# Engine orders rebuilt in a gated attention and feed-forward kernel, with order constraints of the scheduler removed

## The chip, the cores and the metric

The kernel runs on one core of a Trainium2 chip. The metric is the device time of one execution in microseconds (us); lower is better. All executions used here are fast, on a granted clock of 0.998 to 1.0; one execution of the kernel before, of 301.57 us at a clock of 0.853, is left out. A ratio is the mean time of one kernel's fast runs over the mean of the other's fast runs of the same rounds, so it is not quite the ratio of the medians quoted beside it. The *head* is the time before the first score fill, some 15 us. The *span* is what the profiler traces of an execution; the device time was 1.7 us longer in most executions.

## The reference, cut to what matters

```python
# x [1, 2048, 512] bf16, 32 heads of 16, 4 segments of 512 rows; feed-forward width 1792
g = sigmoid((x * gate_w).sum(-1))
for s in range(4):                       # attention with a running memory
    p     = softmax(q_s @ k_s.T * scale + causal_mask)
    a_dot = p @ v_s
    a_mem = (phi(q_s) @ M) / (phi(q_s) @ z + 1e-6)
    o_s   = sigmoid(beta) * a_mem + (1 - sigmoid(beta)) * a_dot
    M, z  = M + phi(k_s).T @ v_s, z + phi(k_s).sum()
a = concat(o_s) @ wo
b = (gelu(x @ w_gate) * (x @ w_up)) @ w_down
return g * a + (1 - g) * b
```

## The kernel before

The program is a set of named tasks. `qk2_1A0` fills the four score banks for one part of query tile 1 of segment 2 (a *fill*), `exp…` is its exponential on ScalarE, `pv` a P*V group, `mz` the memory group of a segment, `K Q V` projections, `G U D` pieces of the gate, up- and down-projection. A piece is two matmuls of 512 columns, 217 ns each from start to start. Pieces are matmuls of 128*128 by the trace's records (*full-array*); fills (32*128), P*V (128*17) and memory groups (128*32) consist of small matmuls (*tiled* work). The order of the tasks on each engine is a fixed list; a list scheduler in the source only plays it through, with its estimates of time, to choose PSUM banks. The semaphore waits are derived from what each task reads and writes.

```python
COLD = 5.8
BLOCK, BLOCK_ASK, BLOCK_END = 256, 165, 208
ORDER = {"pe": ("warm3 warm0 ... qk2_1B1 U2_4.0 U2_4.2 pv2_0_1 mz2 qk2_2A0 D1_3.10 ..."), ...}
HOP = {PE: 0.17, ...}
...
    # the scheduler, on TensorE: two instructions for each matmul
    n_ins = 2 * len(t.alts[PE])
    k = (done + n_ins - BLOCK_END) // BLOCK
    if done < BLOCK_END + BLOCK * k and k - 1 in fetched:
        t.finish = max(t.finish, fetched[k - 1] + ...)
    k = (done + n_ins - BLOCK_ASK) // BLOCK
    if done < BLOCK_ASK + BLOCK * k:
        fetched[k] = t.finish + max(0.8, min(dma_free - t.finish + 0.5, 4.0)) + 2.25
    done += n_ins
...
    for i in range(7):                                   # warm-up before the input has landed
        n = 512 if i < 6 else 384
        task(f"warm{i}", PE, [Instr(lambda e, gw=gw, n=n: e.matmul(
            gw.f32()[:, 0:n], ones[:, 0:128], ones[:, 0:n], start=True, stop=True), [], [gw.key], mm_t(n))], ...)
...
            for sm in sem_out + [sem_tail]:              # the last waits
                e.wait_ge(sm, 16)
```

The four lines around `BLOCK` matter later: the source holds an estimate of how TensorE's instructions arrive. Its figures are the source's own; what the runs show of them comes below.

The softmax here doesn't subtract the row's maximum and nothing guards it: scores larger than these inputs give would overflow.

## Time and profile before

| | before |
|---|---|
| time, median (lowest to highest) | 270.64 us (270.62 to 271.37, 3 runs); in the rounds beside the changed kernel 271.01 us (270.62 to 271.69, 6 runs) |
| span of the profiled run | 268.5 us |
| first score fill, last score fill | 14.79 us, 252.34 us |
| first score fill to end of the last matmul's issue | 250.72 us |
| stalls of TensorE in that stretch | 2.59 us, in 15 places of 0.07 to 0.41 us |
| work of TensorE after the last fill | 13.16 us |

A *stall* is a distance between two starts on TensorE above what the same step takes elsewhere: 217 ns for a matmul of 512 columns, 330 ns for a fill (345 for the low one), 664 ns for a P*V group, 640 ns for a memory group, 312 ns from a full-array matmul of 512 columns to the tiled work behind it, which is 95 ns above 217. The profile lines behind it are in the prediction.

### The profile page before, as it was taken

To read this page: it belongs to the slowest core of one execution; us is meant where nothing else is said; L and a number is where in the kernel's file an instruction comes from. 1 tells how busy PE (TensorE), PEld (TensorE's weight loads), DVE (VectorE), ACT (ScalarE), POOL (GpSimd) and SP (SyncE) were. 2 spreads that over 40 slices of the span, in tenths; PEclk is the share of its full clock that TensorE was granted. 3 is DMA by queue.
4 is the path that set the end of the run, shared out by engine and by line. 5 is a ranking of instruction groups with operands and counts; after the bars stand their busy time and mean duration, and the time that the engine had idled before them with its cause. 6 is when DMAs were issued, how large, how long until landed. Compare 5 with 4: busy or idle time off the path is not lost.

```text
span 268.5 us, 7148 instructions
## 1 busy us (share of the span) xinstructions
PE 263.2 (98%) x3017; PEld 118.9 (44%) x3017; DVE 199.4 (74%) x387; ACT 213.1 (79%) x188; POOL 106.4 (40%) x256
## 2 busy tenths in 40 slices
PE   8999999999999999999999999999999999999995
PEld 4634444344444435444444444443434443444453
DVE  1669888888897778878875987679787756667351
ACT  3899998989999697879968898778795886777702
POOL 8105876733000385253270342428470056344120
DMA  7954247334046135010000314210002023101002
GB/s 214 319 154 80 42 142 167 129 115 104 0 129 110 39 78 142 21 42 2 2 0 2 79 36 86 77 66 1 4 2 61 11 50 38 25 20 42 2 0 78
DMA packets 32815, 18.22 MB, mean 68 GB/s; under 512 B 20624, under 2 KB 32784, under 8 KB 32784
## 3 DMA queue, kind: packets, MB, share of 16 engines
q1 hardware_dynamic: 32208, 17.25, 25.4%
q8 instruction: 23, 0.38, 0.6%
q10 hardware_dynamic: 576, 0.52, 0.6%
q14 instruction: 8, 0.07, 0.1%
HBM read 9.84 MB, written 2.10 MB: 44 GB/s over the span
## 4 chain that ended last, share of the span: by engine, by line
PE 88%; ACT 9%; DMA 1%; issue 1%; POOL 0%; SPq 0%; ACTq 0%
PE psW L498 68%; PE psXALL L864 10%; ACT pt L871 7%; PE psW L914 5%; PE psXALL L498 3%; ACT ptl L871 1%; DMA wk<-in_A_wk_dram 1%; PE psW L922 1%; PE psW L830 1%; POOL ptl L875 0%; ACT ost L1050 0%; PE psXALL L596 0%; SPq L529 0%; ACTq L394 0%
## 5 line engine op out<-in xcount | busy, mean ns | idle before, releaser
L871 ACT ACTIVATE pt<-psXALL 128x2048 bf16<-128x2048 f32 x64 | 120.0, 1875 | 23.5 <-PE psXALL L864 21.4
L875 POOL TENSOR_SCALAR_AFFINE_SELECT pt<-pt 128x256 bf16<-128x256 bf16 x128 | 56.8, 454 | 67.2 <-ACT pt L871 62.4
L498 PE MATMUL psW<-xT,wu 128*128 128x512 bf16 x224 | 54.9, 380 | 0.0
L875 POOL TENSOR_SCALAR_AFFINE_SELECT ptl<-ptl 128x512 bf16<-128x512 bf16 x32 | 23.0, 719 | 77.3 <-ACT ptl L871 75.7
L498 PE MATMUL psW<-xT,wg 128*128 128x512 bf16 x224 | 53.6, 380 | 0.0
L498 PE MATMUL psW<-wd,hT 128*128 128x512 bf16 x210 | 52.5, 380 | 0.0
L1020 DVE TENSOR_TENSOR hT<-psW,hT 128x512 bf16<-128x512 f32 x56 | 36.9, 685 | 12.3 <-PE psW L498 12.1
L929 DVE STREAM_TRANSPOSE tb<-psW 128x512 f32<-128x512 f32 x32 | 21.9, 704 | 17.8 <-PE psW L922 17.5
L498 PEld LDWEIGHTS psW<-xT,wg 128*128 128x128 bf16 x224 | 20.4, 98 | 25.3 <-issue 2.3
L498 PEld LDWEIGHTS psW<-xT,wu 128*128 128x128 bf16 x224 | 20.2, 98 | 24.2 <-issue 2.3
L498 PEld LDWEIGHTS psW<-wd,hT 128*128 128x128 bf16 x210 | 18.6, 98 | 21.4 <-issue 3.0
L864 PE MATMUL psXALL<-qT,kpad 32*128 32x320 bf16 (+3 forms) x512 | 25.4, 273 | 1.4 <-ACT pt L871 0.8
L999 ACT ACTIVATE hT<-psW 128x512 bf16<-128x512 f32 x28 | 15.9, 601 | 7.5 <-PE psW L498 7.5
L871 ACT ACTIVATE ptl<-psXALL 128x2048 bf16<-128x2048 f32 x8 | 15.0, 1877 | 6.1 <-PE psXALL L864 6.0
L914 PE MATMUL psW<-pt,vaug 128*17 128x192 bf16 (+3 forms) x512 | 19.2, 273 | 0.0
L864 PEld LDWEIGHTS psXALL<-qT,kpad 32*128 32x128 bf16 x512 | 7.6, 92 | 24.3 <-ACT pt L871 17.2
L498 PE MATMUL psW<-wv,xT 128*128 128x512 bf16 x64 | 17.0, 380 | 0.0
L498 PE MATMUL psW<-xT,wk 128*128 128x512 bf16 (+1 forms) x80 | 16.7, 337 | 0.2 <-DMA wk<-in_A_wk_dram 0.2
L498 PE MATMUL psW<-wo,oT 128*128 128x512 bf16 x60 | 16.1, 380 | 0.0
L773 POOL COPY exsT<-exs 32x4 f32<-32x4 f32 x64 | 14.4, 225 | 3.7
L914 PEld LDWEIGHTS psW<-pt,vaug 128*17 128x17 bf16 x512 | 10.2, 90 | 12.5 <-issue 4.9
L515 DVE CAST hT<-psW 128x512 bf16<-128x512 f32 x17 | 11.4, 684 | 2.6 <-PE psW L498 2.6
(101 smaller groups left out, 312.7 us busy)
## 6 DMA issues: line engine op xcount, KB each, us to landing
out_dram<-ost SPq DMA_DIRECT2D x15, 128.0 KB, 1.9
wg<-in_B_w_gate_dram SPq DMA_DIRECT2D x2, 896.0 KB, 6.5
wu<-in_B_w_up_dram SPq DMA_DIRECT2D x2, 896.0 KB, 5.1
wd<-in_B_w_down_dram SPq DMA_DIRECT2D x2, 896.0 KB, 5.6
phkt<-in_A_x_dram SPq DMA_DIRECT2D x3, 512.0 KB, 3.6
vlow<-vaug SPq DMA_DIRECT2D x8, 136.0 KB, 2.7
wq<-in_A_wq_dram SPq DMA_DIRECT2D x2, 256.0 KB, 4.7
wv<-in_A_wv_dram SPq DMA_DIRECT2D x2, 256.0 KB, 5.3
```

Of the source, the lines that this page charges most:

```text
L498: return Instr(lambda e: e.matmul(view(), lhsT, rhs, start=first, stop=last), reads=reads, writes=[fkey if fkey is not None else g.key], e ...
L515: alts[DVE] = [Instr(lambda e: e.tensor_copy(dst(), src()), reads=reads, writes=writes, est=dve_t(n))]
L773: cross = task(f"exsT{s}", POOL, [Instr(lambda e, g=g, c=c: e.tensor_copy(exsT[sl][32 * g:32 * g + 32, c:16:4], exs[32 * c:32 * c + 32, s4 ...
L830: Instr(lambda e, t=t, kt=kt, c=c: e.matmul(gm.f32()[32 * c:32 * c + 32, 34 * t:34 * t + 34].rearrange("p (j e) -> p j e", e=17), phkt[:, ...
L864: instrs.append(Instr(lambda e, g=g, lhs=lhs, rhs=rhs, c0=c0, ncol=ncol: e.matmul(X[g][:, c0:c0 + ncol], lhs(32 * g), rhs(32 * g), start=T ...
L871: prev_exp[0] = exp_task(s, f"exp{s}_{t}{name}", [Instr(lambda e: e.activation(dst[:], XALL[:, :].rearrange("p (g c) -> p g c", g=4), ACTF ...
L875: task(f"msk{s}_{t}{name}", POOL, [Instr(lambda e, view=view, pat=pat, base=base: e.affine_select(out=view, in_=view, compare_op=ALU.is_ge ...
L914: instrs.append(Instr(lambda e, t=t, q=q, kb=kb, slot=slot, c0=c0: e.matmul(gp.f32()[32 * q:32 * q + 17, 128 * kb + 64:512], Vaug[sl][:, k ...
L922: instrs.append(Instr(lambda e, t=t, q=q, kb=kb, c0=c0: e.matmul(gp.f32()[32 * q:32 * q + 17, 128 * kb:128 * kb + 64], Vlow[j][:, kb, 4 * ...
L929: task(f"pvt{s}_{t}_{j}", DVE, [Instr(lambda e: e.transpose(Tb[:, j, :], gp.f32()[:, :]), [gp.key], [("Tb", j)], dve_t(512))], grp=gp)
L999: lambda e, g=g, ft=ft, s=s: e.activation(hT[s % 2][:, ft, :], g.f32()[:, :], ACTF.Gelu_apprx_tanh),
L1020: task(f"Um{s}_{ft}", DVE, [Instr(lambda e, g=g, ft=ft: e.tensor_tensor(hT[sl][:, ft, :], g.f32()[:, :], hT[sl][:, ft, :], ALU.mult), [g.k ...
```

## The change

The change frees the order of the tasks from constraints that the data do not ask for, gives new engine lists, corrects constants of the scheduler, and waits for the last 128-column piece of the output last.

```diff
-COLD = 5.8
+COLD = 4.9
 BLOCK, BLOCK_ASK, BLOCK_END = 256, 165, 208
 ORDER = {
-    ... qk2_1B1 U2_4.0 U2_4.2 pv2_0_1 mz2 qk2_2A0 D1_3.10 D1_3.12 D1_3.14 D1_1.0 D1_1.2 qk2_2B0 pv2_1_1 pv2_1_0 ...
+    ... K3_0.0 K3_0.2 qk2_2A0 U2_10.0 U2_10.2 pv2_1_1 mz2 pv2_1_0 qk2_2B0 D1_3.6 D1_3.8 V3_1.0 ...
     ... (the five lists, all rebuilt)
-HOP = {PE: 0.17, ...}
+HOP = {PE: 0.25, ...}
     ... (estimated sizes of ten input transfers)
-                    [("phkt", t), ("Vaug", sl, kt)], [gm.key], 0.009)
+                    [("phkt", t), ("Vaug", sl, kt)], [gm.key], 0.0115)
-                p = task(f"pv{s}_{t}_{j}", PE, instrs, grp=gp, after=joint)
+                p = task(f"pv{s}_{t}_{j}", PE, instrs, grp=gp)
-                mine[0].preds.add(lead)                 # gate groups of a segment, one after the other
-                                        kb == 3, 512) for kb in range(4)], 2, after=[gelu_of[s, ft]])
+                                        kb == 3, 512) for kb in range(4)], 2)
-            dep = hdep + (fins if last else [S._w[("oT", sl, tile, 3)]])
+            dep = fins if on_x else ()
-            for sm in sem_out + [sem_tail]:
+            for sm in sem_out[:-1] + [sem_tail, sem_out[-1]]:
                 e.wait_ge(sm, 16)
```

## The prediction

> **What bounds the kernel now.** I read the page first (engine shares, chain), then the waits, then the chain and the TensorE timeline where the chain leaves TensorE, and last the instruction records themselves, from which I took the start of every matmul and its distance to the next.

> ```profile
> span 268.5 us, 7148 instructions
> PE 263.2 (98%) x3017; PEld 118.9 (44%) x3017; DVE 199.4 (74%) x387; ACT 213.1 (79%) x188; POOL 106.4 (40%) x256
> ...
> PE 88%; ACT 9%; DMA 1%; issue 1%; POOL 0%; SPq 0%; ACTq 0%
> ```

> TensorE is busy 98% of the span and carries 88% of the chain; ScalarE carries 9%. Nothing else matters. The waits say what the 9% is: TensorE (its weight loads) waits for the exponentials that empty the four score banks, and ScalarE waits for the scores that fill them.

> ```profile
> ACT pt L871 <- PE psXALL L864: 21.4, 42, 0.8
> PEld psXALL L864 <- ACT pt L871: 18.0, 42, 0.8
> ```

> A weight load runs ahead of its matmul, so these 18.0 us are mostly hidden. Where they are not, the chain passes through the exponential (last segment):

> ```profile
> 221.83 0.44 PE psXALL L864 x8
> ...
> 222.35 1.89 ACT pt L871
> 224.24 0.05 issue
> 224.28 0.50 PE psXALL L864 x8
> ...
> 224.87 1.89 ACT pt L871
> 226.76 0.05 issue
> 226.80 0.51 PE psXALL L864 x8
> ...
> 227.39 1.89 ACT pt L871
> ```

> Score fills follow each other here at 224.28 and 226.80: 2.52 us, which is the shortest period the single set of score banks allows (exponential 1.89, hop 0.05, fill and hop 0.5 to 0.6). TensorE had less than that to do in between:

> ```profile
> 224.28 0.40 PE L864 MATMUL psXALL<-qT,kpad 32*128 32x320 bf16 x8 [0.17 <-ACT pt L871]
> 224.61 1.04 PE L498 MATMUL psW<-xT,wu 128*128 128x512 bf16 x4
> 225.49 0.59 PE L498 MATMUL psW<-wd,hT 128*128 128x512 bf16 x2
> 226.01 0.61 PE L914 MATMUL psW<-pt,vaug 128*17 128x448 bf16 x16
> 226.45 0.29 PE L922 MATMUL psW<-ptl,vlow 128*17 128x64 bf16 x16
> 226.80 0.40 PE L864 MATMUL psXALL<-qT,kpad 32*128 32x448 bf16 x8
> ```

> Six full-array matmuls and one P*V group end at 226.67 or so; the fill waits for the exponential that ends at 226.75.

> **What TensorE's time consists of.** From the records I took start-to-start distances: 217 ns on average after a 512-column matmul (713 pairs), 60 ns after one of 136 columns, one fill of the four score banks 330 ns (345 for the low fill), one P*V group 664 ns, two in a row 1217 ns for both (so 553 for the first), a memory group 640 ns, and 107 ns lost each time a full-array matmul is followed by a fill or a group. Counting the program's order with these: 1033 full-array matmuls 205.6 us; 77 entries into tiled work 8.2; 72 fills 23.9; P*V groups 22 x 664 + 10 x 553 = 20.1; 3 memory groups 1.9; sum 259.7 us. Measured from the first matmul (0.84) to the end of the last one's issue (265.50) are 264.7 us. The difference of 5.0 us has two parts. The head: warm-up matmuls 427 ns apart instead of 216, then waits for the first rows of wk, 2.4 us. Stalls later: 1.7 us in the steps from full-array work to a fill above the 107 ns, 0.6 us in steps from P*V to a fill that took up to 797 ns instead of 664, 0.15 us at 196.8 us, and 0.2 us in memory groups beside a P*V group (up to 751 ns); about 2.5 us in all. After the last matmul come 0.6 us of eviction, the output transfer (issued 266.39, landed 268.00) and the final waits: 2.9 us.

> So everything that an order of instructions can still win is 2.5 us of stalls, some tenths in the head, and a part of the 259.7. That is at most 1.2% of the time.

> [...] a 512-column matmul counts 380 ns, yet the next starts after 217, so 98% busy hides the stalls above and I used starts. [...] The kernel gives four to the scores and four to everything else; this limits how early an up-projection may start, as it holds its bank until its gelu is there.

> **The change part by part.** *Order constraints removed.* They are arguments of the scheduler only; the orders are fixed lists, and semaphore waits are derived from the data, so no instruction and no necessary wait disappears. They matter by what they allow: an up-projection before its gelu, a down-projection that starts with the hidden tiles that are ready, P*V groups two in a row. *Engine orders.* The same 625 TensorE tasks. The number of entries into tiled work is 77 again; P*V groups that directly precede another group rise from 10 to 13, so 3 x 111 ns = 0.33 us go: 259.4 us. *Spacing of the fills.* With the costs above I summed the TensorE work between each fill and the next. A fill period under 2.52 us (2.46 if full-array work precedes the fill, since 217.23 to 219.69 is such a pair) leaves TensorE waiting. Before there are 13 such intervals, 8 of them in the last segment, from 2.16 to 2.49 us; their deficits sum to 1.6 us of the 2.5 us measured. After there are three: 2.37 us (fill 1_1B1 to 1_2A0), 2.18 (3_2L to 3_2A1), 2.40 (3_3A1 to 3_3B1), deficits 0.09 + 0.28 + 0.06 = 0.43 us. The work that fills them is taken from the end: after the last fill 11.7 us of TensorE work remain instead of 13.1. So 1.6 - 0.43 = 1.2 us go. *The other 0.9 us of stalls* come from an exponential that starts late: at 188.31 one started 0.87 us after its fill instead of 0.59, and in the first segment copies sit between exponentials (57 to 63 us). The new lists move copies into longer intervals (3.58 us where three copies follow one exponential), so I let a third of it go, 0.3 us. *Head.* A seventh K-projection matmul hides part of a wait for the second half of the input (landed at 5.59 and 5.79): 0.1 us. All four first evictions are now on VectorE, 0.4 us each, in time for their readers by my count. *Tail.* One of the four last evictions goes to VectorE; the last piece's eviction did not wait in the trace (0.12 us after its matmul), so nothing is won. *Final waits.* The profile has them in pairs, the 384-column piece's last but one; waiting for the 128-column piece last may let one more already satisfied wait (0.06 us each in the trace) come after the landing: +0.06 us. *Model constants* (cold start, hop, transfer sizes) reach no instruction except through the choice of banks.
> Sum: 0.33 + 1.2 + 0.3 + 0.1 - 0.06 = 1.9 us. 270.64 - 1.9 = 268.8 us, 0.7% less.

> **Rivals.** *A: bank waits take the place.* Gates and up-projections are now opened earlier and hold banks longer: before the fourth fill (around 22 us) I count four open groups, one waiting for VectorE until about 22.7 us, just when the next group wants a bank. For: VectorE is 74% busy, and the slack there is about zero by my count. Against: in the trace of before, which has equally dense stretches, just one bank-like stall (0.14 us at 196.8) shows. It would cost 0.5 to 1.5 us and leave 269.3 to 270.3. *B: the fill period is ScalarE's, not TensorE's.* If the evictions moved between exponentials (two or three of 0.59 us) make ScalarE the bound in the first segment, stalls of 0.1 to 0.4 us appear at each; intervals of 2.60 us with a 1.05 us exponential task of the feature map in between need 2.85 us, but each is followed by one of 2.95 or more. Result 269 to 269.5. *C: all stalls vanish* and the head gains: 267.7 at the least. *D: transfers.* The memory group of the first segment moves from 38.6 to about 33 us; its transposes landed at 33.65. VectorE finishes their source some 3 us earlier by the new list, so they should land near 30.5; if not, TensorE stalls up to 1 us there.

> **Range and chances.** From C at 267.7 to A and D together at 270.3; the runs of before spread by 0.3% at most. I take 267.8 to 270.1. A change of 2% (5.4 us) is twice all that is idle, so faster than that has 1%; slower by 2% would need a blocked order, 1%.

> **What would show it right or wrong.** Right: steps from full-array work to a fill of 107 ns nearly throughout, the last fill some 1.5 us earlier relative to the end, the period of score fills in the last segment 2.6 us with ScalarE's wait for scores up and TensorE's for the exponential down; chain share of the exponentials from 7% to some 3%. Wrong: TensorE waiting for evictions (VectorE or ScalarE tiles) at 20 to 25 or 65 to 75 us, a wait for the transposed features near 33 us, or a fresh stall at the start of the down-projections.

0.33 + 1.2 + 0.3 + 0.1 - 0.06 us come to 1.87, its 1.9 us, and 270.64 less that is its 268.8 us. How far a weight load runs ahead of its matmul can be read in the trace of the kernel before: it starts 214 ns earlier in the median of the full-array matmuls and 27 ns in that of the tiled ones, at most 217 ns. What the rivals would cost are estimates.

## The result

The changed kernel took 269.83 us (median of 6; 268.92 to 270.22), the kernel before 271.01 us in the same rounds. The ratio is 0.9951, with a 95% interval of 0.993 to 0.9973: within 2%, and inside the predicted range. The predicted 268.8 us was 1.0 us too low.

These are the engine and chain shares of the changed kernel's page:

```profile
span 268.1 us, 7137 instructions
...
PE 262.9 (98%) x3017; PEld 118.9 (44%) x3017; DVE 200.7 (75%) x390; ACT 208.8 (78%) x184; POOL 105.9 (39%) x256
...
PE 96%; ACT 2%; issue 1%; DVE 0%; ACTq 0%
```

TensorE now carries 96% of the chain (the work that ended last, followed back) instead of 88%, and ScalarE 2% instead of 9%. The view of the waits, for the same two pairs as before and one further row (engine, line, tile, what was waited for: us in all, times, longest):

```profile
ACT pt L871 <- PE psXALL L864: 24.8, 41, 2.4
...
PEld psXALL L864 <- ACT pt L871: 17.4, 41, 0.6
...
PEld psXALL L864 <- issue: 3.8, 7, 1.3
```

ScalarE waits 3.4 us more for scores and TensorE's weight loads 0.6 us less for exponentials, which is the intended exchange. The last row is not intended. In the kernel before it is 3.0 us, 7 times, at most 0.4; now one score fill has a weight load that waited 1.3 us for "issue", that is for nothing the profile shows. The chain in the last segment, where the kernel before went through an exponential every 2.52 us (start, us, engine, tile and line, instructions):

```profile
217.41 0.33 PE psXALL L864 x8
217.74 2.27 PE psW L498 x10
220.00 0.33 PE psXALL L864 x8
220.33 2.26 PE psW L498 x10
222.60 0.33 PE psXALL L864 x8
```

Fills come every 2.60 us with ten full-array matmuls between them, and here the chain no longer leaves TensorE. Between the first fill and the last matmul it passes through an exponential only three times, at 105.5, 238.6 and 251.4 us, which are the three short intervals that the prediction had counted. The shortest, before fill 3_2A1:

```profile
238.11 0.48 PE psXALL L864 x32
238.59 0.02 issue
238.61 1.89 ACT ptl L871
240.50 0.05 issue
240.54 0.40 PE psXALL L864 x8
```

The stalls of the changed kernel in the stretch from first fill to last matmul are 0.14 us at 107.4, 0.06 at 152.0, 1.33 at 174.8, 0.19 at 197.7, 0.06 at 230.3, 0.32 at 240.5 and 0.13 at 253.3; in all 2.24 us. Without the third they are 0.91 us. That third one is here, in TensorE's timeline of the changed kernel (start, us, engine, line, operation, tiles, shape, count, in brackets the idle time before it and its releaser):

```profile
172.13 0.81 PE L830 MATMUL psW<-vaug,phkt 128*32 128x34 bf16 x64
172.77 0.63 PE L914 MATMUL psW<-pt,vaug 128*17 128x448 bf16 x16
173.21 0.30 PE L922 MATMUL psW<-ptl,vlow 128*17 128x64 bf16 x16
173.44 0.31 PE L864 MATMUL psXALL<-qT,kpad 32*128 32x320 bf16 x3
174.79 0.37 PE L864 MATMUL psXALL<-qT,kpad 32*128 32x320 bf16 x5 [1.04 <-issue]
```

Three of eight matmuls of one fill, then nothing for a microsecond, then the other five. The profile names no releaser, and in the program that the source builds only the first matmul of this fill carries a semaphore wait, so data and banks do not explain it. In front of it stand P*V, memory group, P*V and fill in one row, with no full-array matmul between: 272 instructions of TensorE, weight loads included, in about 2 us. The queues of the page name the candidate (packets, MB, share of 16 engines' span):

```profile
q8 instruction: 23, 0.38, 0.6%
```

These are 23 packets of 16,384 bytes for TensorE's 6034 weight loads and matmuls. 6034 / 23 is 262, so one packet brings, by estimate, about 260 instructions; the kernel's source has 256 for it (`BLOCK`). In the trace's transfer records one of them starts at 172.21 us, in the middle of that row of work.

So the result has this account. From first fill to last matmul the profiled runs need 250.72 us before and 250.39 us after, 0.33 us less, although 1.7 us of the old stalls are gone: 1.3 us came back in one place. With 0.10 us less before the first fill and 0.05 us more after the last matmul, the two profiled executions differ by 0.38 us of time (270.21 and 269.83). The medians differ by 1.2 us. Where the rest lies is not shown, as the other executions have no profile. Two things vary by as much: the head (the profiled run of before had the earliest first fill, 14.79 us, of the four profiles that have its lists or nearly so, 14.79 to 15.99), and the time outside the traced span.

### The profile page after: what moved, and what is told of

Same layout as the page of the kernel before. It is cut to its first block, busy times and chain, and to the rows that moved or that the text cites. A ratio compares the mean times of both kernels' runs of the same rounds, so it can differ in the third digit from the quotient of the medians.

```text
span 268.1 us, 7137 instructions
## 1 busy us (share of the span) xinstructions
PE 262.9 (98%) x3017; PEld 118.9 (44%) x3017; DVE 200.7 (75%) x390; ACT 208.8 (78%) x184; POOL 105.9 (39%) x256
## 4 chain that ended last, share of the span: by engine, by line
PE 96%; ACT 2%; issue 1%; DVE 0%; ACTq 0%
PE psW L498 75%; PE psXALL L864 9%; PE psW L914 6%; PE psXALL L498 3%; ACT pt L871 1%; PE psW L922 1%; PE psW L588 1%; ACT ptl L871 1%; PE psW L830 0%; PE psXALL L596 0%; ACT ost L1043 0%; DVE xT L604 0%; ACTq L394 0%
## 5 line engine op out<-in xcount | busy, mean ns | idle before, releaser
L871 ACT ACTIVATE pt<-psXALL 128x2048 bf16<-128x2048 f32 x64 | 120.1, 1876 | 26.7 <-PE psXALL L864 24.8
L875 POOL TENSOR_SCALAR_AFFINE_SELECT pt<-pt 128x256 bf16<-128x256 bf16 x128 | 58.2, 465 | 74.9 <-ACT pt L871 70.2
L498 PE MATMUL psW<-xT,wu 128*128 128x512 bf16 x224 | 56.7, 380 | 0.0
L498 PE MATMUL psW<-wd,hT 128*128 128x512 bf16 x210 | 54.1, 380 | 0.0
L498 PE MATMUL psW<-xT,wg 128*128 128x512 bf16 x224 | 53.9, 380 | 0.0
L1014 DVE TENSOR_TENSOR hT<-psW,hT 128x512 bf16<-128x512 f32 x56 | 37.5, 688 | 20.1 <-PE psW L498 19.9
L498 PEld LDWEIGHTS psW<-xT,wu 128*128 128x128 bf16 x224 | 20.3, 98 | 25.2 <-issue 2.7
L498 PEld LDWEIGHTS psW<-xT,wg 128*128 128x128 bf16 x224 | 20.4, 98 | 24.6 <-issue 1.9
L498 PEld LDWEIGHTS psW<-wd,hT 128*128 128x128 bf16 x210 | 18.7, 98 | 21.6 <-issue 2.1
L864 PE MATMUL psXALL<-qT,kpad 32*128 32x320 bf16 (+3 forms) x512 | 25.7, 273 | 1.4 <-issue 1.0
L998 ACT ACTIVATE hT<-psW 128x512 bf16<-128x512 f32 x28 | 15.3, 601 | 8.1 <-PE psW L498 8.0
L864 PEld LDWEIGHTS psXALL<-qT,kpad 32*128 32x128 bf16 x512 | 7.7, 92 | 26.2 <-ACT pt L871 16.1
L914 PE MATMUL psW<-pt,vaug 128*17 128x192 bf16 (+3 forms) x512 | 18.9, 273 | 0.0
L871 ACT ACTIVATE ptl<-psXALL 128x2048 bf16<-128x2048 f32 x8 | 15.0, 1876 | 4.2 <-PE psXALL L864 4.0
L498 PE MATMUL psW<-xT,wk 128*128 128x512 bf16 (+1 forms) x80 | 17.5, 349 | 0.1
L498 PE MATMUL psW<-wv,xT 128*128 128x512 bf16 x64 | 16.6, 380 | 0.0
L498 PE MATMUL psW<-wo,oT 128*128 128x512 bf16 x60 | 16.4, 380 | 0.0
L914 PEld LDWEIGHTS psW<-pt,vaug 128*17 128x17 bf16 x512 | 10.3, 90 | 10.4 <-issue 2.7
L773 POOL COPY exsT<-exs 32x4 f32<-32x4 f32 x64 | 13.1, 204 | 4.0 <-ACT exs L764 0.4
L498 PE MATMUL psW<-xT,wq 128*128 128x512 bf16 x48 | 13.5, 381 | 0.0
```

The source lines that it names most:

```text
L498: return Instr(lambda e: e.matmul(view(), lhsT, rhs, start=first, stop=last), reads=reads, writes=[fkey if fkey is not None else g.key], e ...
L773: cross = task(f"exsT{s}", POOL, [Instr(lambda e, g=g, c=c: e.tensor_copy(exsT[sl][32 * g:32 * g + 32, c:16:4], exs[32 * c:32 * c + 32, s4 ...
L864: instrs.append(Instr(lambda e, g=g, lhs=lhs, rhs=rhs, c0=c0, ncol=ncol: e.matmul(X[g][:, c0:c0 + ncol], lhs(32 * g), rhs(32 * g), start=T ...
L871: prev_exp[0] = exp_task(s, f"exp{s}_{t}{name}", [Instr(lambda e: e.activation(dst[:], XALL[:, :].rearrange("p (g c) -> p g c", g=4), ACTF ...
L875: task(f"msk{s}_{t}{name}", POOL, [Instr(lambda e, view=view, pat=pat, base=base: e.affine_select(out=view, in_=view, compare_op=ALU.is_ge ...
L914: instrs.append(Instr(lambda e, t=t, q=q, kb=kb, slot=slot, c0=c0: e.matmul(gp.f32()[32 * q:32 * q + 17, 128 * kb + 64:512], Vaug[sl][:, k ...
```

## The experiments

**e0_after_again: the changed kernel unaltered.**

> The changed kernel unaltered. Its profile showed one stall of 1.33 us inside a score fill (third to fourth matmul, 173.4 us), with no semaphore behind it, just after a 16 KB packet on the instruction queue. Fetch theory (TensorE ran out of fetched instructions because P*V, memory group, P*V and the fill are 272 instructions in 1.9 us): the stall is there again at the same instruction, 0.8 to 1.5 us. Rival (an accident of that execution): it is absent or elsewhere. Head: the first fill started at 14.69 us, though one V matmul pair fewer lies ahead of it than in the kernel before (14.79); [...] the first fill moves by some tenths here; if it is the order, it stays at 14.6 to 14.8. Ratio to before 0.993 to 0.997.

270.41 us, ratio 0.9986 (0.9961 to 1.0011). First fill 15.48 us instead of 14.69, first fill to last matmul 250.44 us instead of 250.39, and the pause again inside the same fill, after its third matmul, with 1.39 us between the two starts. So the pause is no accident of one execution. The head is: it moved by 0.8 us, more than the tenths that were expected, and TensorE sat idle for 1.24 us for a transfer of x. The ratio misses the expected 0.993 to 0.997, and its interval includes no gain at all. For the changed order alone the gain over the kernel before is then 0.1 to 0.5%.

**e1_mz_apart: the memory group taken out of the row.**

```diff
- U2_10.2 pv2_1_1 mz2 pv2_1_0 qk2_2B0 D1_3.6 D1_3.8 V3_1.0 D1_3.10
+ U2_10.2 pv2_1_1 pv2_1_0 qk2_2B0 D1_3.6 D1_3.8 V3_1.0 mz2 D1_3.10        (and VectorE's tasks to match)
```

> The changed kernel with one task moved: the memory group of the third segment goes from between two P*V groups to after the third matmul pair of the next interval, and its VectorE accumulation one place later. Fetch theory: the stall of 1.3 us is gone, no new one of over 0.3 us near it, the time falls by 1.0 to 1.4 us less 0.1 us for one more entry into tiled work; ratio to before 0.990 to 0.992. Rival (something at that fill, score banks or data, holds TensorE): the stall stays at the same fill, ratio 0.995.

269.39 us, ratio 0.9956 (0.9931 to 0.9981). The pause is gone, and first fill to last matmul takes 249.28 us, 1.16 us less than in e0. Its first fill was as late as 15.96 us, which is why the span shows less. The stretch fell as expected; the ratio, expected at 0.990 to 0.992, did not, and two of its six times lie 2.9 us above their span instead of 1.7. This speaks against data as the cause, but not yet for blocks: the input load had moved too, to 176.77 us.

**e5_tail: the shortest interval lengthened.** One piece is pulled ahead through each of the last fills, so that the interval before 3_2A1 has ten full-array matmuls.

```diff
- D2_1.4 D2_2.12 qk3_2A1 D2_1.6 D2_1.8        (and so on through six fills, to the end)
+ D2_1.4 D2_2.12 D2_1.6 qk3_2A1 D2_1.8
```

> The changed kernel, in its last segment: one matmul pair moved ahead into the interval of 2.18 us and each later fill behind one pair more, so that work is taken from the end. Spacing theory: the stall of 0.32 us before that fill is gone and comes nowhere else, 0.3 us less (ratio 0.994 against 0.995 of the changed kernel). Rival (the end is bound by the chain after the last exponential): the stall is gone but as much is lost between the last fill and the last matmul, time as for the changed kernel.

269.57 us, ratio 0.996 (0.994 to 0.9979). The stall of 0.31 us that e0 has before 3_2A1 is gone and none came in its place. First fill to last matmul is 250.40 us all the same, as in e0, because the pause was 1.68 us in this execution instead of 1.39. The step is right, the total hid it.

**e7_uneven: six intervals made short.** A fill is moved ahead of a piece at six places, so that the interval behind it is longer and that before it short by one piece.

```diff
- D0_1.2 D0_1.4 qk1_1B1 mz1
+ D0_1.2 qk1_1B1 D0_1.4 mz1        (likewise 2_1B1, 2_2L, 2_2B1, 3_0L, 3_0B1)
```

> The changed kernel with six fills put one matmul pair earlier, so that six intervals of 2.60 us become 2.17 and the next one longer by 0.43; no work or entry added. Spacing theory: six stalls of 0.29 us (2.46 less 2.17), 1.75 us more than the changed kernel, ratio to before about 1.0015. Rival (the order's gain lies elsewhere: pairs of P*V, evictions, transfers): under 0.5 us more.

272.22 us, ratio 1.0048 (1.0026 to 1.007). Six new stalls of 0.28 to 0.36 us, 2.0 us in all, and first fill to last matmul 252.79 us, 2.35 us more than e0; the remaining 0.36 us are a longer pause. That is a little more than the 1.75 us and the ratio of 1.0015 that were expected. The chain shows one of them in its form (start, us, what), the fill at 222.28 released by an exponential and 12 matmuls behind it:

```profile
220.35 1.89 ACT pt L869
222.24 0.05 issue
222.28 0.40 PE psXALL L862 x8
222.68 2.70 PE psW L496 x12
```

So the same work, with the same mean distance of fills, costs what each short interval lacks, and the longer interval behind it gives nothing back.

**e3_old_orders: everything of the change but the lists.**

```diff
  (the changed kernel)
-ORDER = {new lists}
+ORDER = {lists of the kernel before}
```

> Everything of the change but the engine orders: the order constraints are gone, the constants are new, the last output piece is awaited last, but the five lists are those of the kernel before. Theory (the prediction's): the constraints and constants reach no instruction, only the lists do; a comparison of the built programs shows all five engines' streams and waits equal to the kernel before except the pairing of the last waits. So the ratio to the kernel before is 1.000 within 0.002, first score fill to last matmul 250.7 us as before, the same 2.6 us of stalls at the same score fills, and from the landing of the last output to the end of the span 0.06 us more. Rival (the freed scheduling or the constants themselves save time, through the choice of banks): ratio 0.998 or less, and the stalls of before partly gone.

270.84 against 270.92 us, ratio 0.9995 (0.9972 to 1.0018). Stalls of 2.48 us at the same fills, first fill to last matmul 250.61 us, first fill at 15.99 us, 1.2 us later than in the same order's other profile. Constraints and constants alone do nothing, as the prediction said; only the lists reach the chip.

**e4_burst_in_before: the row of small matmuls put into the kernel before.**

```diff
- pv2_0_1 mz2 qk2_2A0 D1_3.10 D1_3.12 D1_3.14 D1_1.0 D1_1.2 qk2_2B0 pv2_1_1 pv2_1_0
+ pv2_0_1 qk2_2A0 D1_3.10 D1_3.12 D1_3.14 D1_1.0 D1_1.2 qk2_2B0 pv2_1_1 mz2 pv2_1_0        (and VectorE's tasks to match)
```

> The kernel before with one piece of the new order alone: the third memory group goes between two P*V groups, so that 256 small matmuls and a score fill follow each other without a full-array matmul. Theory (TensorE's instruction fetch falls behind in such a run, and how far depends on where the fetch packet falls): a pause of about 0.8 us (0.5 to 1.3) without a semaphore in or just behind that run, near 175 to 177 us, absent in the kernel before; one P*V group fewer starts behind other work (0.1 us won); ratio 1.002 to 1.005. Rival (the pause in the changed kernel had another cause, or needs its exact neighbours): no such pause, ratio 0.999 to 1.001.

273.73 us, ratio 1.0113 (1.0091 to 1.0135), so slower than I expected, and for other reasons. There is no pause without a releaser in the row or behind it: both expectations of the theory fail in this form. Instead TensorE waits at 172.0 (0.50 us, the interval that lost the memory group is now short), inside the row at 176.6 (0.43 us, for VectorE's transposition of a P*V result), at 181.2 (0.94 us, for a copy on ScalarE) and at 183.7 us (1.66 us). The chain of the last one:

```profile
176.93 5.98 DMA out_dram<-ost
182.91 0.03 issue
182.94 0.76 DVE ost L1069
183.69 0.05 issue
183.74 2.33 PE psW L497 x10
```

The memory group is the last reader of the tile `phkt`. Moved back by 4 us, it let the 512 KB load of the next segment's input into that tile start at 176.46 instead of 172.16 us; an output transfer was issued behind it, at 176.93, and took 5.98 us (the median of its kind is 1.9 us on the page of the kernel before), VectorE waited 4.80 us for its staging tile, and TensorE 1.59 us for VectorE. The experiment was not the isolated one I meant it to be. What it left of theory F was that a row of small matmuls alone is not enough; then its place in the blocks has to matter.

**e6_best: three edits of the list together.** As e1 and e5, with one piece also pulled ahead through fills 1_2A0 to 1_3B1.

> The changed kernel with three edits of its TensorE list: the third memory group is moved away from the two P*V groups, the short interval before fill 3_2A1 is lengthened, and one matmul is pulled ahead through the fills 1_2A0 to 1_3B1 so that the shortest interval of segment 1 is lengthened too. Theory (the fetch pause and the short intervals are separate and add): first score fill to last matmul 248.8 us (against 250.4 in the changed kernel and 250.7 before), made up of 1.1 us for the pause and 0.3 and 0.1 us for the intervals; the pauses at 107 us and 240 us gone; ratio to the kernel before 0.990 to 0.993. Rival (what is won at one place is waited for at the next fill): 249.3 us or more, ratio 0.995 or above, as with the first edit alone.

269.06 us, ratio 0.9939 (0.9921 to 0.9958); first fill to last matmul 249.15 us. The pause and the stalls at 107 and 240 us are gone, as expected, but there is a new stall of 0.28 us at 133.9 us, among the gate pieces of the next segment, so 0.35 us of the expectation are missing. There a piece waits for a gelu on ScalarE; the exponential in front of that gelu started 0.3 us later than in the changed kernel, counted from the first fill. By ratio it misses what I had written; the edit in segment 1 is not worth having.

**The place in the blocks.** I then counted. In the changed kernel the pause lies before matmul 2000 of the program (counted from 0), and the 128 matmuls before it, 256 instructions with their loads, take 1.87 us without the pause, one of the shortest such stretches of the program. If block ends lie there, and every 128 matmuls from there, the lists need not be touched to move the pause. It is enough to add matmuls at the start. Three runs do that with the warm-up:

```diff
         n = 512 if i < 6 else 384
+        if i == 5:                                       # the first in the list; 3 in the kernel before
+            task(f"warm{i}", PE, [Instr(lambda e, gw=gw, j=j: e.matmul(
+                gw.f32()[32 * (j % 4):32 * (j % 4) + 32, 16 * (j // 4):16 * (j // 4) + 16], ones[:, 0:32],
+                ones[:, 0:16], start=True, stop=True, tile_position=(0, 32 * (j % 4))),
+                [], [gw.key], 0.01) for j in range(33)], ...)      # 33 (e9), 9 (e8, e12b), 93 (e10)
+            continue
```

**e9_shift32: the changed kernel, all later matmuls 32 places later.**

> As the run before, with 33 small warm-up matmuls in place of one, so that all later matmuls come 32 later in the program; order untouched. Theory: no block of 128 matmuls that ends at a block end takes less than 5.1 us now, so there is no pause at all; first score fill to last matmul 249.1 us (248.9 to 249.4), like the run in which the memory group was moved away (249.3), ratio 0.993 to 0.997; the three short intervals keep their waits of 0.06 to 0.32 us. Rival: the pause of 1.0 to 1.7 us stays, 250.4 us.

268.56 us, ratio 0.9926 (0.9911 to 0.994), and first fill to last matmul 249.08 us. TensorE's timeline at the same row of work:

```profile
172.10 0.81 PE L836 MATMUL psW<-vaug,phkt 128*32 128x34 bf16 x64
172.75 0.63 PE L920 MATMUL psW<-pt,vaug 128*17 128x448 bf16 x16
173.18 0.30 PE L928 MATMUL psW<-ptl,vlow 128*17 128x64 bf16 x16
173.42 0.40 PE L870 MATMUL psXALL<-qT,kpad 32*128 32x320 bf16 x8
```

The fill runs through. The order and the row of work are those of the changed kernel, and the input load behind the memory group starts at 173.07 us, where it started at 173.09; only the warm-up and the count in front have changed. Rival S falls. The ratio is slightly better than the expected 0.993 to 0.997. The other stalls are the old ones to a hundredth (0.15, 0.06, 0.19, 0.07, 0.32, 0.13 us).

**e8_shift8: 8 places later.**

> The changed kernel, order untouched; the first of its seven warm-up matmuls (512 columns) is replaced by nine of 16 columns on a quarter of the columns of the array, so that every later matmul is the eighth-later one in the program. Theory (TensorE's instructions come in blocks of 256, that is 128 matmuls with their weight loads; the pause is at matmul 2000, the end of a block; two ends must be 3.2 us apart or TensorE waits for the rest): the block that ended there now ends at old number 1992 and takes 2.81 us by the trace of the changed kernel instead of 1.87, so the pause shrinks from 1.3 to about 0.4 us (0.2 to 0.8) and is found at old number 1992, inside the second P*V group; first score fill to last matmul 249.5 (249.3 to 249.9), ratio 0.995 to 0.998. Rival (the pause belongs to this sequence of work, or to the input load that starts there): still 1.3 us at the same matmul, inside the fill, 250.4 us.

The timeline has the pause inside the second P*V group, five matmuls before its end:

```profile
173.37 0.27 PE L928 MATMUL psW<-ptl,vlow 128*17 128x64 bf16 x11
173.91 0.22 PE L928 MATMUL psW<-ptl,vlow 128*17 128x64 bf16 x5 [0.28 <-issue]
```

By count it stands before matmul 2000 of the new program, number 1992 of the old: the pause stayed with the count and left its work. Start to start it is 0.47 us, first fill to last matmul 249.73 us. So far as expected. The times are not: 271.60 us in the median (269.92 to 272.90, 4 runs), ratio 1.0054 (1.0028 to 1.008), where 0.995 to 0.998 was expected. The profiled run was the fastest of the four. Part of the excess lies outside the traced span: it is 1.8 to 2.8 us in these four executions (mean 2.5) and 1.8 us in the mean of the kernel before in the same rounds.

**e12b_shift8_again: the same kernel once more.**

> The same kernel as the run with nine small warm-up matmuls, once more, as its profile showed the expected short pause of 0.45 us at matmul 2000 and 249.7 us from first fill to last matmul, but three of its four times lay 1.6 to 3 us above the profiled one. If those times were the head [...] or chance, the median comes out at 269.5 to 270.5, ratio 0.995 to 1.000; if they belong to this kernel, the median is again 271.5 or more, ratio 1.004 or above, and the profile then shows where.

270.45 us (269.71 to 271.39), ratio 0.9983 (0.9965 to 1.0001). So most of the excess did not come back. And this profile, of the same program, shows the pause at the same matmul, with another length:

```profile
174.37 0.27 PE L928 MATMUL psW<-ptl,vlow 128*17 128x64 bf16 x11
175.70 0.22 PE L928 MATMUL psW<-ptl,vlow 128*17 128x64 bf16 x5 [1.06 <-issue]
```

1.25 us from start to start instead of 0.47, with the first fill at 15.85 instead of 14.65 us: two things that vary by 2.0 us together from one execution to the next. The 272.90 us of one execution of e8 (span 270.1 us) go beyond that; it has no profile, and its cause stays open.

**e10_shift92_before: the kernel before, all later matmuls 92 places later.** Its own row of P*V, memory group, P*V at 102 us does no harm there. Here it is laid into one block.

> The kernel before, order untouched, with 93 small warm-up matmuls in place of one, so that its own run of P*V, memory group, P*V near 102 us falls into one block: by its trace that block of 128 matmuls takes 1.99 us. Theory: a pause of 3.2 - 2.0 = 1.2 us (0.9 to 1.6) without a semaphore appears at old matmul 1140, the score fill right behind that run near 104 us, where the kernel before has none; nowhere else is there a new one, as the next shortest block takes 5.2 us; first score fill to last matmul 251.9 us (251.5 to 252.3) against 250.7; the head may be up to 1 us longer or shorter by the other warm-up; ratio 1.002 to 1.008. Rival: no pause, 250.7 us.

271.48 us, ratio 1.0035 (1.0021 to 1.0049), first fill to last matmul 251.38 us, 0.66 us more than before. The pause is there:

```profile
104.31 0.40 PE L870 MATMUL psXALL<-qT,kpad 32*128 32x448 bf16 x8
104.64 0.39 PE L498 MATMUL psW<-xT,wu 128*128 128x512 bf16 x1
105.63 1.67 PE L498 MATMUL psW<-xT,wu 128*128 128x512 bf16 x7 [0.60 <-issue]
```

It came six matmuls later than I had counted and was smaller, 0.78 us above the usual distance instead of 1.2, so that the stretch misses the expected 251.5 to 252.3 us as well. The six matmuls have a cause: semaphore instructions take places too. By the trace 32 of them (one a drain at the start) have gone by at matmul 2000 of the changed kernel and 20 at matmul 1238 here. 2 x 2000 + 32 is 4032, and 2 x 1238 + 20 is 2496; both leave 192 when divided by 256. All pauses of which the trace has every record, three programs in four executions, lie on this one count.

**What sets its length.** For each pause, from the records (times in us; "block end before" is the start of the matmul 128 places earlier):

| run | block end before | packet starts | TensorE goes on | end to packet | packet to going on |
|---|---|---|---|---|---|
| after | 171.58 | 172.21 | 174.79 | 0.63 | 2.58 |
| e0 | 172.37 | 173.03 | 175.63 | 0.66 | 2.60 |
| e5 | 171.72 | 173.00 | 175.27 | 1.28 | 2.27 |
| e7 | 172.65 | 173.89 | 176.26 | 1.25 | 2.37 |
| e8 | 170.64 | 171.28 | 173.91 | 0.64 | 2.63 |
| e12b | 171.64 | 173.40 | 175.70 | 1.76 | 2.30 |
| e10 | 102.77 | 103.02 | 105.63 | 0.25 | 2.61 |

From the packet's start to the next instruction it is 2.3 to 2.6 us in all seven. What varies is when the packet starts, here 0.25 to 1.76 us after the start of the matmul at the block end before it. That corrects the fixed 3.2 us of my expectations (1.87 and 1.33), and explains why one program has a pause of 0.47 and of 1.25 us.

The length of a block alone does not decide. By the same count the changed kernel has a second short block, from 32.12 to 34.89 us (the first memory group and two P*V groups): 2.77 us, as short as the one with a pause in e8, and TensorE runs through it. Its packet had started at 30.55 us, 1.57 us before the block's first matmul and 4.34 us before the first of the next block. Over the 23 block ends of this profile the packet starts between 1.9 us before and 2.4 us after that matmul. So what counts is the time from the packet's start to the start of the first matmul behind the next block end. In the ten profiles with every record it is under 2.7 us only at the four pauses (2.29 to 2.63 us, the pause included), and 2.76 us or more at every other block end from the second on, none of which has a pause without a releaser. The smallest of these are 2.76 us in e6, 3.42 in the kernel before and 3.65 in e4; in e9 it is nowhere under 6.77. Why the packet starts sooner or later is not settled; no run here isolates it.

**e11b_shift_tail: e9 and e5 together.**

> The changed kernel with the two repairs that the earlier runs found good: 33 small warm-up matmuls in place of one (all later matmuls 32 later in the program), and the short interval before fill 3_2A1 lengthened by pulling one matmul ahead through the last fills. Theory: the two are separate and add; no pause at matmul 2000, no wait at 240 us; first score fill to last matmul 249.08 - 0.32 = 248.76 us (248.6 to 249.0), ratio 0.990 to 0.993, the fastest of the study. Rival (the wait of 0.32 us comes back at a later fill): 249.1 us.

268.57 us, ratio 0.9913 (0.9899 to 0.9927), first fill to last matmul 248.75 us against the expected 248.76. The two repairs add. This is the fastest kernel by ratio: 0.9% under the kernel before, where the change alone has 0.1 to 0.5%.

## Why the prediction was right, and which step it lacked

- **Range.** 267.8 to 270.1 us hold the 269.83. With the pause out of the way (e9) the same lists took 268.56 us beside 270.49 for the kernel before: 1.93 us less, where the prediction's sum was 1.9; by the interval of the ratio it is 1.6 to 2.4 us, and e9 also has another first warm-up, so the agreement to hundredths is chance. That 269.83 lies in the range is partly luck too: the room above 268.8 had been left for rivals A and D, which did not come, and something else took it. The same kernel measured again (e0, 270.41 us) lies above the range, in rounds in which the kernel before took 270.67.
- **TensorE's work, 0.33 us less.** Right. Stalls taken off, first fill to last matmul is 248.13 us before and 248.16 us in e9. The new order has one more piece, 0.43 us, behind the first fill instead of ahead of it, so like for like it is 0.40 us less.
- **Spacing of the fills.** Right, and the best of its steps. The three intervals left, with deficits of 0.09, 0.28 and 0.06 us, are the three places where fills wait, at 107.4, 240.5 and 253.3 us, with 0.14, 0.32 and 0.13. After the last fill 11.74 us of work remain, as counted (11.7). With the third of the other stalls that was let go, 1.5 of 2.5 us should vanish; 1.67 of 2.59 us did (0.92 left in e9). (The four parts of the stalls in the prediction add up to 2.65 us, not to its "about 2.5".) e5 and e7 show the rule from both sides.
- **Constraints and constants.** Right: e3.
- **Head.** The first fill came 0.1 us earlier in the two profiles compared, but not as argued, and it proves nothing: ten profiles with the new lists have it between 14.65 and 15.96 us, four with the old between 14.79 and 15.99. The first evictions on VectorE were not in time for their readers: a weight load of the first projection waited 0.4 us for one.
- **Tail and final waits.** Right: one more satisfied wait after the last landing, and 3.02 us from the last matmul's issue to the end instead of 2.97.
- **Rivals.** None came. There is no wait for banks at 20 to 25 or 65 to 75 us, and the memory group at 33 us starts without a wait.
- **The step that failed** is the sum itself, "0.33 + 1.2 + 0.3 + 0.1 - 0.06 = 1.9 us": it held what the new order takes away and no term for what an order can add other than waits for data, banks and engines. The missing term is 1.3 us of instruction arrival. The signs of being wrong named waits for evictions, for the transposed features and at the start of the down-projections, not one inside a score fill.

The kernel's source had pointed there. Its scheduler plays through block ends at 208, 464, … of its own count, two for each matmul, and would have put the ends around this row five matmuls before the end of the first P*V group and 19 matmuls behind the fill, inside the next one; the stretch between, by the changed kernel's trace and without the pause, takes about 4.0 us. The measured end is at 160 in that count, 24 matmuls earlier, and there the block takes 1.87 us. Of these 48 instructions, 32 are the semaphore instructions (and the drain) gone by until then, which the model's count leaves out. If the lists were made with this model, it took the worst place for a tolerable one. That is read from the source and the trace; no run made new lists with a corrected count.

## What to carry to other kernels

When an order of instructions is all that changes, add the work between two dependent stages and compare it with the period that the other engine needs: in e7 each shortfall of 0.29 us cost 0.28 to 0.36 us, and the surplus behind it paid nothing back. If a pause splits one group of matmuls in the middle and has no releaser, count instructions (loads and semaphores included) to it from the start and look for a fixed distance, as here 192 above a multiple of 256; adding some empty work at the start then tells a matter of place from a matter of data in one run, and may already be the repair. Judge gains of half a percent by a stretch of the trace that leaves out the head, when, as here, the head alone moves by 1.3 us (14.65 to 15.99) and the time outside the span by another 1.3 (1.7 to 3.05).
